# Starting the first two column pairs together, seven products each in turns, in a split-float32 kernel

## The chip, the cores and the metric

One core of a Trainium2 chip runs the kernel. The metric is the device time of one execution in microseconds; the time before is the median of three runs, 792.79 us (792.09 to 792.79). One further execution was taken with the hardware profiler.

## What is computed

The reference takes x (2048 tokens by 512), two DFT matrix pairs and three weights, and returns a mix of two branches per token:

```python
x = A_x
g = _sigmoid((x * gate_w).sum(-1, keepdims=True))
# branch a: y = Real(DFT_seq(DFT_hidden(x)))
a = einsum("bsd,ed->bse", x, dft_hid_re);  b = einsum("bsd,ed->bse", x, dft_hid_im)
y = einsum("ts,bse->bte", dft_seq_re, a) - einsum("ts,bse->bte", dft_seq_im, b)
# branch b: gate = relu(x @ W_gate), up = x @ W_up, out = (gate * up) @ W_down   (F = 1792 columns)
return g * y + (1 - g) * out
```

Everything is float32. The change lies in the first part of branch b, the products of x with `W_gate` and `W_up`.

## The kernel before

**Numbers.** TensorE multiplies values of a rounded kind (F32R). To keep float32 accuracy each operand is split into a hi part (a cast by ACT, in some places by DVE) and a lo part (operand minus hi, a subtraction on DVE), and each product is made of three matmuls, the pairs in `PARTS = ((1, 0), (0, 1), (0, 0))`: lo by hi, hi by lo, hi by hi. So every operand costs one ACT and one DVE operation before TensorE can use it.

**Blocks.** Where it can, the kernel multiplies two by two block matrices with seven products in place of eight (`LEFT`, `RIGHT`: which sums of blocks go into product m). For branch b the right side is x transposed: its blocks "11", "21", "12", "22" are (half of the 512 inputs, half of the tokens of a group q), each 128 partitions by 2 by 512. The left side is a pair of columns c of the weights (two 128-column tiles of `W_gate` and of `W_up`; seven pairs in all): four blocks, for gate and up (index i). Product 1 is block 11 by block 11, product 2 is block 12 by x's "21", products 3 to 7 need sums or differences on at least one side: 5 needs x "12" minus "11" and a weight sum, 6 adds x "22", and so on. The class `Weights` (line 403) loads and splits a pair's weights; `Block` (line 478) runs the seven products of one pair and one token group in the order 1, 5, 6, 2, 7, 3, 4, each 12 matmuls (i, inner half k, part), 84 in all. `evac` reads the banks between them: ACT copies what product 1 left into a second pair of banks, where 6 and 7 add to it, ACT keeps copies for later sums, and DVE forms h = relu(gate) times up. The eight PSUM banks are four pairs named x, m, y and t (line 342).

**The start.** The first column pair of the first token group is done in another way, by the class `Direct` (line 533): eight plain block products straight from the raw blocks, 96 matmuls, with its own copy of these weights (`wf`). It starts with 15 matmuls on a constant tile (`warm_up`, line 978) while the first loads travel. Then x's blocks come in the order "11", "21" (each in two halves, between pieces of `wf`), "12", "22", then the weights of pair 1 (`w1`, lines 985 to 1013). Meanwhile DVE and ACT split pair 1's weights and build x's sums for `Block(1, 0)`, the next in the `sequence` (line 1018). Its split weights are stored to HBM (`keep`) through POOL's queue and fetched again for the second token group at the end of branch b's first part. Then follow pairs 2 to 6 for both token groups, the spectral blocks, the two pairs left over (`tail`), the down projection (`Down`) and the sequence transform (`Sequence`, `Joint`).

**What sets the order.** Nothing is issued as it is written. Every operation is put down with a key (`op`, `pe`: `plan.now` counts matmuls), and `Plan` (lines 128 to 274) sorts the operations by key, gives DVE's and ACT's a due time from what TensorE needs, and lays them out with a small cost table (0.22667 us per matmul, 2.5 us for a landing, and so on). This fixes the order of each engine's instructions; on the chip each engine then runs its list in order and waits on semaphores. All loads go through SP's queue, at most eight at a time; stores go through POOL's. All compute instructions stand on the one source line 125, so the profile is read by tile names: `xb11h` and `xb11l` are hi and lo of x's block "11", `wf0h` the direct weights, `wa`, `wb` the split weights of products 1, 2, 4 and of 5, 6, 7, 3, `ws` and `xs` the sums, `ps` PSUM.

Of the kernel before, what the change touches and what calls it, by code (L numbers as in the profile page):

```python
# [14 lines left out]
P = 128  # L15
# [11 lines left out]
ORDER = (1, 5, 6, 2, 7, 3, 4)  # L27
BANK = {1: "x", 2: "x", 5: "m", 3: "m", 6: "y", 7: "y", 4: "t"}
# [99 lines left out]
class Plan:  # L128
# [4 lines left out]
    MATMUL, WAIT, LANDING = 0.22667, 0.035, 2.5  # L133
# [56 lines left out]
    def order(self):  # L190
# [12 lines left out]
        while any(todo.values()):  # L203
# [74 lines left out]
def kernel(ctx: ExitStack, tc, xP, xG, wf, wgu, wd, cr, ci, wri, gw, out):  # L278
# [34 lines left out]
    wb = hbm("wb", 8, P, 4, 2, P)  # L313
# [87 lines left out]
    SLOT = {1: 0, 2: 1, 4: 2, 5: 0, 6: 1, 7: 2, 3: 3}  # L401

    class Weights:
        def __init__(self, c):
            self.c = c
            self.raw = [buf(f"wr{i}", [4, 2, P]) for i in range(2)]
            self.sum = [buf(f"ws{i}", [4, 2, P]) for i in range(2)]
            self.a = [[buf(f"wa{i}{x}", [3, 2, P], F32R) for x in "hl"] for i in range(2)]
            self.b = [[buf(f"wb{i}{x}", [4, 2, P], F32R) for x in "hl"] for i in range(2)]

        def load(self, i):
            load(self.raw[i].all, wgu[self.c, i])

        def a_hi(self, i):
            E().scalar.copy(self.a[i][0].all, self.raw[i][:, :3])

        def a_lo(self, i):
            E().vector.tensor_sub(self.a[i][1].all, self.raw[i][:, :3], f32(self.a[i][0].all))

        def b_sum(self, i):  # L420
            r, o = self.raw[i], self.sum[i]
            E().vector.tensor_add(o[:, 0], r[:, 3], r[:, 2])
            E().vector.tensor_sub(o[:, 1], o[:, 0], r[:, 0])
            E().vector.tensor_sub(o[:, 2], r[:, 0], r[:, 3])
            E().vector.tensor_sub(o[:, 3], r[:, 1], o[:, 1])

        def b_hi(self, i):
            E().scalar.copy(self.b[i][0].all, self.sum[i].all)

        def b_lo(self, i):  # L430
            E().vector.tensor_sub(self.b[i][1].all, self.sum[i].all, f32(self.b[i][0].all))

        def keep(self, key):
            for n, t in enumerate(y for x in (self.a, self.b) for i in x for y in i):
                k = t.shape[0]
                op(key + 3 * n, lambda n=n, t=t, k=k: store(wb[n, :, :k], f32(t.all)))

        def fetch(self, key):
            for n, t in enumerate(y for x in (self.a, self.b) for i in x for y in i):
                k = t.shape[0]  # L440
                op(key + 6 * n, lambda n=n, t=t, k=k: load(f32(t.all), wb[n, :, :k]))

        def of(self, m, i):
            return [t[:, SLOT[m]] for t in (self.a if m in (1, 2, 4) else self.b)[i]]

    def w_prep(w, key, ahead=66):
        for i in range(2):
            op(key - ahead + 6 * i, w.load, i)
            op(key - 36 + 12 * i, w.a_hi, i)
            op(key - 30 + 12 * i, w.a_lo, i)  # L450
            op(key - 40 + 12 * i, w.b_sum, i)
            op(key - 34 + 12 * i, w.b_hi, i)
            op(key - 26 + 12 * i, w.b_lo, i)
# [24 lines left out]
    class Block:  # L478


        def __init__(self, q, w):
            self.q, self.w = q, w
# [48 lines left out]


    class Direct:
        def __init__(self):
            self.x = {b: [buf(f"xb{b}{x}", dtype=F32R) for x in "hl"] for b in ("11", "21", "12", "22")}

            self.raw = [buf(f"wf{d}", [2, 4, P]) for d in range(2)]
            self.w = [[buf(f"wf{d}{x}", [2, 4, P], F32R) for x in "hl"] for d in range(2)]
            self.g = [buf(f"dg{j}") for j in range(2)]
            self.h = [buf(f"h{d}") for d in range(2)]  # L540
            self.ps = {(f, j): Pair(2 * j + f) for f in range(2) for j in range(2)}

            for d in range(2):
                for k in range(2):
                    for n in range(3):
                        for i in range(2):
                            pe(2, self.products, [(d, i, f, 0, k, n) for f in range(2)])
                            if d == k == 1 and n == 2:
                                for f in range(2):
                                    op(plan.now, self.evac, f, i, 0)  # L550
            for d in range(2):
                for i in range(2):
                    for f in range(2):
                        pe(6, self.products, [(d, i, f, 1, k, n) for k in range(2) for n in range(3)])
                        if d == 1:
                            op(plan.now, self.evac, f, i, 1)
            h_out(0, 0, self.h, plan.now + 200)

        def products(self, all):
            for d, i, f, j, k, n in all:  # L560
                first = d == k == n == 0
                a, b = PARTS[2 - n]
                mm(self.ps[f, j][i], self.w[d][a][:, k, 2 * i + f], self.x["12"[d] + "12"[j]][b][:, k],
                   start=first, stop=d == k == 1 and n == 2)

        def w_load(self, d, k, n=slice(0, 4)):
            load(self.raw[d][:, k, n], wf[d, :, k, n])

        def w_split(self, d, k, n=slice(0, 4)):
            hi, lo = self.w[d]  # L570
            E().scalar.copy(hi[:, k, n], self.raw[d][:, k, n])
            E().vector.tensor_sub(lo[:, k, n], self.raw[d][:, k, n], f32(hi[:, k, n]))

        def x_split(self, b, k=slice(0, 2), hi=None):
            x, raw = self.x[b], piece[0, b]
# [575 lines left out]
```

## Time and profile before

| what | value |
|---|---|
| median of the runs shown | 792.79 us |
| the profiled execution's own time | 792.87 us |
| its span on the core | 790.8 us |
| granted TensorE clock over the span | 0.998 |
| matmuls in the trace | 3447 |
| HBM read, written | 123.99 MB, 60.83 MB |

The span is what the trace covers; the execution's time has about 2 us beside it. Engines are PE (TensorE), PEld (its weight loads), DVE, ACT, POOL and SP. In a timeline row stand the start, the duration, engine and line, the operation, out<-in with the shape, the count, and in brackets how long the engine was idle before it and what ended that. In a table by stage each row gives a window, then busy time and count for PE, PEld, DVE, ACT and POOL, the granted clock, the share of the DMA engines and GB/s.

### The profile page before, as it was taken

Reading aid. Unit: us, or ns where it says so; the run is one execution under the profiler, and the core shown is the slowest. Engines: PE = TensorE matmul, PEld = TensorE weight load, DVE = VectorE, ACT = ScalarE, POOL = GpSimd, SP = SyncE. Lnnn points to the kernel's source line nnn. Section 1 sums busy time; section 2 is a strip of 40 time slices with the busy share of each in tenths; the row PEclk is TensorE's granted clock in tenths of the full one; section 3 lists DMA queues with packets and bytes.
Section 4 is the critical chain, followed back from the end, with each engine's and each line's share of the span. In section 5 each row is a group of like instructions: output and inputs, shape, how many; then the busy total and the mean of one; then the engine's idle time right before and its main releaser. Section 6 shows DMA issues by size and latency. Waiting matters only on the chain.

```text
span 790.8 us, 9436 instructions
## 1 busy us (share of the span) xinstructions
PE 783.8 (99%) x3447; PEld 647.6 (82%) x3447; DVE 618.7 (78%) x680; ACT 388.6 (49%) x429; POOL 96.8 (12%) x143
## 2 busy tenths in 40 slices
PE   9999999999999999999999999999999999999997
PEld 8888888888888888888888888888788888878885
DVE  7987776767769314978765799967999999989963
ACT  5653333434245334576545474544747355574540
POOL 1102221212212111010000000200011001000200
PEclk9999999999999999999999999999999999999999
DMA  8615777575966984388588789859999889699914
GB/s 321 251 41 194 263 288 253 213 256 200 340 215 218 356 318 174 120 281 292 184 269 312 278 304 323 191 182 293 349 330 279 247 263 187 196 340 333 242 33 80
DMA packets 56750, 193.84 MB, mean 245 GB/s; under 512 B 6656, under 2 KB 6912, under 8 KB 56704
## 3 DMA queue, kind: packets, MB, share of 16 engines
q1 hardware_dynamic: 37840, 124.55, 45.4%
q0 software_dynamic: 18864, 68.69, 29.2%
q8 instruction: 27, 0.44, 0.2%
q14 instruction: 19, 0.16, 0.1%
HBM read 123.99 MB, written 60.83 MB: 234 GB/s over the span
## 4 chain that ended last, share of the span: by engine, by line
PE 94%; DVE 2%; issue 1%; ACT 1%; DMA 1%; SPq 0%; DVEq 0%
PE ps L125 94%; DMA wf<-wf 1%; ACT jch L125 1%; SPq L125 0%; DVE xs L125 0%; DVE ws L125 0%; DVE xl L125 0%; DVE h L125 0%; ACT ps L125 0%; DVE v L125 0%; DVE z L125 0%; DVE wb1l L125 0%; DVE wb0l L125 0%; ACT xh L125 0%; ACT js L125 0%
## 5 line engine op out<-in xcount | busy, mean ns | idle before, releaser
L125 PE MATMUL ps<-ch,lh 128*128 128x512 f32 x580 | 225.6, 389 | 0.0
L125 PE MATMUL ps<-cl,lh 128*128 128x512 f32 x580 | 225.6, 389 | 0.0
L125 PE MATMUL ps<-ch,ll 128*128 128x512 f32 x580 | 225.6, 389 | 0.0
L125 ACT CAST ch<-r 128x1024 fp32r<-128x1024 f32 x96 | 97.5, 1052 | 73.2 <-DVE r L125 60.2
L125 PEld LDWEIGHTS ps<-ch,ll 128*128 128x128 f32 x580 | 108.9, 188 | 22.7
L125 PEld LDWEIGHTS ps<-cl,lh 128*128 128x128 f32 x580 | 108.9, 188 | 22.7
L125 PEld LDWEIGHTS ps<-ch,lh 128*128 128x128 f32 x580 | 108.9, 188 | 22.4
L125 DVE TENSOR_TENSOR cl<-r,ch 128x1024 fp32r<-128x1024 f32 x96 | 114.5, 1220 | 1.1 <-ACT ch L125 0.6
L125 DVE TENSOR_TENSOR cl<-hr,ch 128x1024 fp32r<-128x1024 f32 (+1 forms) x56 | 59.4, 1087 | 18.7 <-ACT ch L125 17.0
L125 ACT ACTIVATE ps<-ps 128x1024 f32<-128x1024 f32 (+1 forms) x33 | 31.6, 956 | 84.2 <-PE ps L125 38.4
L125 ACT COPY s<-ps 128x1024 f32<-128x1024 f32 x42 | 42.6, 1014 | 54.0 <-PE ps L125 52.4
L125 ACT CAST ch<-hr 128x1024 fp32r<-128x1024 f32 (+1 forms) x56 | 51.7, 945 | 26.5 <-PE ps L125 21.2
L125 DVE TENSOR_TENSOR r<-r,r 128x1024 f32<-128x1024 f32 x48 | 57.1, 1218 | 0.0
L125 POOL DMA_DIRECT2D out<-z x23 | 17.1, 743 | 322.5 <-DVE z L125 322.5
L125 DVE TENSOR_TENSOR ll<-l,lh 128x1024 fp32r<-128x1024 f32 (+1 forms) x26 | 30.4, 1168 | 16.1 <-ACT lh L125 14.2
L125 DVE TENSOR_TENSOR u<-ps,s 128x1024 f32<-128x1024 f32 x26 | 31.6, 1220 | 12.1 <-PE ps L125 8.3
L125 DVE TENSOR_TENSOR jcl<-jc,jch 128x1024 fp32r<-128x1024 f32 x28 | 32.8, 1221 | 7.0 <-ACT jch L125 6.5
L125 ACT COPY ps<-ps 128x1024 f32<-128x1024 f32 x17 | 17.0, 998 | 40.3 <-PE ps L125 29.8
L125 PE MATMUL ps<-xh,wb0l 128*128 128x512 f32 x92 | 35.9, 390 | 0.2 <-ACT ps L125 0.2
L125 PE MATMUL ps<-xl,wb0h 128*128 128x512 f32 x92 | 35.8, 389 | 0.0
L125 PE MATMUL ps<-xh,wb1h 128*128 128x512 f32 x92 | 35.8, 389 | 0.0
L125 PE MATMUL ps<-xh,wb0h 128*128 128x512 f32 x92 | 35.8, 389 | 0.0
(219 smaller groups left out, 1404.0 us busy)
## 6 DMA issues: line engine op xcount, KB each, us to landing
hr<-hd SPq DMA_DIRECT2D x42, 512.0 KB, 4.5
r<-cr SPq DMA_DIRECT2D x32, 512.0 KB, 5.7
r<-ci SPq DMA_DIRECT2D x32, 512.0 KB, 6.0
hd<-hs POOLq DMA_DIRECT2D x28, 512.0 KB, 5.0
out<-z POOLq DMA_DIRECT2D x23, 512.0 KB, 6.7
td<-jt POOLq DMA_DIRECT2D x16, 512.0 KB, 4.2
ad<-a POOLq DMA_DIRECT2D x16, 512.0 KB, 5.1
l<-ad SPq DMA_DIRECT2D x16, 512.0 KB, 7.3
```

The source lines that it names most:

```text
L125: getattr(getattr(nc, self.engine), self.name)(*map(ap, self.a), **{k: ap(x) for k, x in self.k.items()})
```

## The change

- `Direct` goes, with its weights `wf`. Column pairs 0 and 1 of the first token group are both run as `Block`s with seven products, in turns: product 1 of pair 0, product 1 of pair 1, product 2 of pair 0, and so on, in the order 1, 2, 5, 6, 3, 7, 4 (`ORDER_S`). Each block has two pairs of PSUM banks; what was in x, m and t shares one pair.
- The loads come in the order that this needs: x "11" in two halves between two pieces of pair 0's block 11, pair 1's block 11, x "21" whole, both pairs' second blocks, x "12", both pairs' other two blocks, x "22".
- Products 1 and 2 of pair 0 go k by k, and hi by hi first (`one` with `first=2`, `n` in 2, 1, 0). x "21" is loaded in one piece and split in two halves (`x_half`).
- `Weights` keeps gate and up side by side: one tile for hi and one for lo of products 1 and 2, one tile `wd` for product 4, and `wb` in two halves. The sums are made product by product over 512 columns; a pair's sums are four DVE operations, not eight. Seven tiles are kept in HBM in place of eight.
- The planner's cost table multiplies a load's time by 2.3 if it is issued between 2.3 and 2.9 us. The warm-up matmuls write the two pairs of banks that product 1 is copied into.

```diff
 ORDER = (1, 5, 6, 2, 7, 3, 4)
+ORDER_S = (1, 2, 5, 6, 3, 7, 4)
 BANK = {1: "x", 2: "x", 5: "m", 3: "m", 6: "y", 7: "y", 4: "t"}
 FIRST = (1, 5)
...
-    MATMUL, WAIT, LANDING = 0.22667, 0.035, 2.5
+    MATMUL, WAIT, LANDING, COLD = 0.22667, 0.035, 2.5, 2.3
...
-                line = max(line, free[s.engine]) + s.work
+                line = max(line, free[s.engine]) + s.work * (self.COLD if 2.3 < t < 2.9 else 1)
...
-    wb = hbm("wb", 8, P, 4, 2, P)
+    wb = hbm("wb", 7, P, 2, 2, 2, P)
...
-    SLOT = {1: 0, 2: 1, 4: 2, 5: 0, 6: 1, 7: 2, 3: 3}
+    SLOT = {1: 0, 2: 1, 5: 0, 6: 1, 7: 2, 3: 3}
+            self.raw = [buf(f"wr{h}", [2, 2, 2, P]) for h in range(2)]
+            self.sum = [buf(f"ws{h}", [2, 2, 2, P]) for h in range(2)]
+            self.a = [buf(f"wa{x}", [2, 2, 2, P], F32R) for x in "hl"]
+            self.d = buf("wd", [2, 2, 2, P], F32R)
+            self.b = [[buf(f"wb{h}{x}", [2, 2, 2, P], F32R) for x in "hl"] for h in range(2)]
+        def load(self, h, n=slice(0, 2), k=slice(0, 2)):
+            load(self.raw[h][:, n, k], wgu[self.c, h, :, n, k])
+        def a_hi(self, n=slice(0, 2), k=slice(0, 2)):
+            E().scalar.copy(self.a[0][:, n, k], self.raw[0][:, n, k])
+        def a_lo(self, n=slice(0, 2), k=slice(0, 2)):
+            E().vector.tensor_sub(self.a[1][:, n, k], self.raw[0][:, n, k], f32(self.a[0][:, n, k]))
+        def d_hi(self):
+            E().scalar.copy(self.d[:, 0], self.raw[1][:, 0])
+        def d_lo(self):
+            E().vector.tensor_sub(self.d[:, 1], self.raw[1][:, 0], f32(self.d[:, 0]))
+        def b_sum(self, m):
+            (a, b), (c, d) = ([r[:, n] for n in range(2)] for r in self.raw)
+            o = [self.sum[n // 2][:, n % 2] for n in range(4)]
+            combine(o[SLOT[m]], *{5: (d, c, 1), 6: (o[0], a, -1), 7: (a, d, -1), 3: (b, o[1], -1)}[m])
+        def b_hi(self, h, n=slice(0, 2)):
+            E().scalar.copy(self.b[h][0][:, n], self.sum[h][:, n])
+        def b_lo(self, h, n=slice(0, 2)):
+            E().vector.tensor_sub(self.b[h][1][:, n], self.sum[h][:, n], f32(self.b[h][0][:, n]))
+        def all(self):
+            return *self.a, self.d, *self.b[0], *self.b[1]
+            for n, t in enumerate(self.all()):
+                op(key + 3 * n, lambda n=n, t=t: store(wb[n], f32(t.all)))
+            for n, t in enumerate(self.all()):
+                op(key + 6 * n, lambda n=n, t=t: load(f32(t.all), wb[n]))
+        def of(self, m, i, k):
+            if m == 4:
+                return [self.d[:, n, k, i] for n in range(2)]
+            n = SLOT[m]
+            return [t[:, n % 2, k, i] for t in (self.a if m < 3 else self.b[n // 2])]
...
+        for h in range(2):
+            op(key - ahead + 6 * h, w.load, h)
+            for m in ((5, 6), (7, 3))[h]:
+                op(key - 40 + 10 * h, w.b_sum, m)
+            op(key - 34 + 10 * h, w.b_hi, h)
+            op(key - 27 + 10 * h, w.b_lo, h)
+        op(key - 36, w.a_hi)
+        op(key - 30, w.a_lo)
+        op(key + 20, w.d_hi)
+        op(key + 26, w.d_lo)
...
-        def __init__(self, q, w):
-            self.q, self.w = q, w
+        def __init__(self, q, w, banks=PAIRS):
+            self.q, self.w, self.banks = q, w, banks
             self.g = {r: buf("g" + r, (N,)) for r in ("11", "21")}
             self.s = {m: buf(f"s{m}") for m in (5, 6)}
             self.u = {r: buf("u" + r) for r in ("12", "22")}
             self.h = [buf(f"h{d}") for d in range(2)]
+        def run(self):
             for m in ORDER:
                 for i in range(2):
                     pe(6, self.product, m, i)
                 self.evac(m, plan.now)
-            h_out(q, w.c, self.h, plan.now + (8 if plan.now > 270 else 100))
+            self.done(plan.now + (8 if plan.now > 270 else 100))
+        def done(self, key):
+            h_out(self.q, self.w.c, self.h, key)
         def product(self, m, i):
-            w, x, ps = self.w.of(m, i), X[self.q, m], PAIRS[BANK[m]]
-            n = 0
             for k in range(2):
-                for a, b in PARTS:
-                    mm(ps[i], w[a][:, k], x[b][:, k], start=m in FIRST and n == 0, stop=n == 5)
-                    n += 1
+                for n in range(3):
+                    self.one(m, i, k, n)
+        def one(self, m, i, k, n, first=0):
+            w, x, ps = self.w.of(m, i, k), X[self.q, m], self.banks[BANK[m]]
+            a, b = PARTS[n]
+            mm(ps[i], w[a], x[b][:, k], start=m in FIRST and k == 0 and n == first,
+               stop=m in (2, 3, 4, 7) and k == 1 and n == 2 - first)
         def evac(self, m, key):
-            x, y, p, t = (PAIRS[k] for k in "xymt")
+            x, y, p, t = (self.banks[k] for k in "xymt")
...
-    class Direct:
...
-            mm(ps8[:, 6, :N // 2], warm[:, :P], warm.all, start=n == 0, stop=n == WARM - 1)
+            half = slice(n % 2 * (N // 2), (n % 2 + 1) * (N // 2))
+            mm(ps8[:, (2, 3, 6, 7)[n // 2 % 4], half], warm[:, :P], warm.all, start=n in (0, 2, 4, 6), stop=True)
-    w1, direct = Weights(1), Direct()
+    ws = [Weights(c) for c in range(2)]
+    for m in (1, 2, 3, 5, 6, 7, 4):
+        x_raw(0, m)
+    halves, whole = [slice(0, 1), slice(1, 2)], slice(0, 2)
+
+    def x_half(m, k, hi=None):
+        h, l, raw = (t[:, k] for t in X[0, m])
+        (hi or E().scalar.copy)(h, raw)
+        E().vector.tensor_sub(l, raw, f32(h))
+
+    def w_half(w, n, k=whole):
+        w.a_hi(n, k)
+        w.a_lo(n, k)
+
+    for k in halves:
+        op(-99, x_load, 0, "11", k)
+        op(-99, ws[0].load, 0, halves[0], k)
+    op(-99, ws[1].load, 0, halves[0])
+    op(-99, x_load, 0, "21")
+    for w in ws:
+        op(-99, w.load, 0, halves[1])
+    op(-98, x_load, 0, "12")
+    for w in ws:
+        op(-98, w.load, 1)
+    op(-98, x_load, 0, "22")
+    op(-98, lambda: load(gwt[:], gw))
+    for k in halves:
+        op(-90, x_half, 1, k, plan.vector.tensor_copy)
+        op(-90, w_half, ws[0], halves[0], k)
+    op(-90, w_half, ws[1], halves[0])
+    op(-90, x_half, 2, halves[0])
+    op(-90, w_half, ws[0], halves[1])
+    op(-90, x_half, 2, halves[1])
+    op(-90, w_half, ws[1], halves[1])
+    for n, m in enumerate((5, 6, 3, 7, 4)):
+        key = 24 * n + 20
         for f, *a in ((x_sum, 0, m), (hi_of, X[0, m]), (lo_of, X[0, m])):
+            op(key, f, *a)
+        for w in ws:
+            if m == 4:
+                op(key, w.d_hi)
+                op(key, w.d_lo)
+            else:
+                h, i = divmod(SLOT[m], 2)
+                op(key, w.b_sum, m)
+                op(key, w.b_hi, h, halves[i])
+                op(key, w.b_lo, h, halves[i])
+
+    start = [Block(0, w, {k: Pair(2 * c + (k == "y")) for k in "xymt"}) for c, w in enumerate(ws)]
+    for m in ORDER_S:
+        for b in start:
+            if m in (1, 2) and b is start[0]:
+                for k in range(2):
+                    for n in (2, 1, 0):
+                        for i in range(2):
+                            pe(1, b.one, m, i, k, n, 2)
+            else:
+                for i in range(2):
+                    pe(6, b.product, m, i)
+            b.evac(m, plan.now)
+    for b in start:
+        b.done(plan.now + 100)
+    ws[1].keep(plan.now)
+    w = ws[1]
...
-    sequence = [(1, 0), (2, 0), (2, 1)]
+    sequence = [(2, 0), (2, 1)]
...
-            Block(q, w)
-            if (c, q) == (1, 0):
-                w.keep(plan.now - 40)
+            Block(q, w).run()
...
-        b = w.reshape(2, 2, P, KF // 2, 2, P).transpose(3, 2, 4, 0, 1, 5)
-        return np.stack([b[:, :, 0, 0], b[:, :, 0, 1], b[:, :, 1, 1], b[:, :, 1, 0]], axis=2)
+        return w.reshape(2, 2, P, KF // 2, 2, P).transpose(3, 0, 4, 2, 1, 5)
-    wgu = np.stack([blocks(wg), blocks(wu)], axis=1)
-
-    first = wgu[0][:, :, [[0, 3], [1, 2]]].transpose(2, 1, 4, 0, 3, 5).reshape(2, P, 2, 4, P)
+    wgu = np.stack([blocks(wg), blocks(wu)], axis=5)
+    wgu = np.stack([np.stack([wgu[:, 0, 0], wgu[:, 1, 0]], axis=2), np.stack([wgu[:, 1, 1], wgu[:, 0, 1]], axis=2)], axis=1)
-        "wf": laid(first),
```

More of the change, by code (lines that the diff above doesn't have):

```diff
@@ L277, with kernel @@
 @with_exitstack
-def kernel(ctx: ExitStack, tc, xP, xG, wf, wgu, wd, cr, ci, wri, gw, out):
+def kernel(ctx: ExitStack, tc, xP, xG, wgu, wd, cr, ci, wri, gw, out):
     nc = tc.nc
@@ L405, in __init__ @@
             self.c = c
[L406 to L428, printed above, removed]
@@ L530, in evac @@
                 rectified("21", 0, t, -1.0)
-    class Direct:
[L534 to L575, printed above, removed]
-            (hi or E().scalar.copy)(x[0][:, k], raw[:, k])
-            E().vector.tensor_sub(x[1][:, k], raw[:, k], f32(x[0][:, k]))
-        def evac(self, f, i, j):
-            g, ps = self.g[j][:, f], self.ps[f, j]
-            if i == 0:
-                E().scalar.activation(g, ps[0], AF.Relu)
-            else:
-                E().vector.tensor_mul(self.h[f][:, j], g, ps[1])
```

42 lines of the change are left out of this document (removed).

## The prediction

> **What bounds the kernel now.** I read the page first, then the chain that ended last in order of time.
>
> ```profile
> span 790.8 us, 9436 instructions
> ...
> PE 783.8 (99%) x3447; PEld 647.6 (82%) x3447; DVE 618.7 (78%) x680; ACT 388.6 (49%) x429; POOL 96.8 (12%) x143
> ```
> ```profile
> 0.74 0.39 SPq L125
> ...
> 4.50 6.52 DMA wf<-wf
> ...
> 33.10 519.88 PE ps L125 x2291
> ```
>
> The page alone says "TensorE is busy 99%". The chain says more: up to 33.10 us it runs through other work, the first loads among it (issued from 0.74 on), and after that through matmuls alone, 2291 of them in 519.88 us, so 0.2269 us each. From 33.10 on only the number of matmuls counts. Before it, what counts is when the operands of the first products are ready. The change acts on both. The table by stage says the same of the later part:
>
> ```profile
> 200.00:780.00 580.00, 579.52 (x2554) 478.68 (x2553) 462.74 (x468) 300.93 (x326) 60.63 (x82) 1.00 0.80 253
> ```
>
> TensorE is busy in 579.52 of 580.00 us, at a granted clock of 1.00. Now the landmarks of the stretch that is rewritten, from the timeline:
>
> ```profile
> 4.59 1.96 PE L125 MATMUL ps<-xb11h,wf0h 128*128 128x512 f32 x4
> ...
> 10.95 1.07 PE L125 MATMUL ps<-xb21h,wf1h 128*128 128x512 f32 x4
> ...
> 32.48 0.39 PE L125 MATMUL ps<-xh,wb1h 128*128 128x512 f32 x1
> ...
> 33.10 0.50 PE L125 MATMUL ps<-xh,wb0l 128*128 128x512 f32 x1 [0.23 <-ACT ps L125]
> ...
> 46.83 0.39 PE L125 MATMUL ps<-xb11h,wa0l 128*128 128x512 f32 x1
> ```
>
> The first real matmul starts at 4.59. The first one that reads x's second block is the 25th and starts at 10.95. Between 32.48 and 33.10 TensorE loses 0.62 - 0.23 = 0.39 us, waiting for ACT's copy of a bank; and since 33.10 + 60 x 0.2269 would be 46.71, another 0.12 just after it. At 46.83 the first matmul of column pair 2 starts: pairs 0 and 1 are through for the first half of the tokens. That is the point at which I compare, since nothing after it changes in kind.
>
> **Fewer matmuls.** Pair 0 is computed directly now:
>
> ```profile
> L125 PE MATMUL ps<-xb12h,wf0h 128*128 128x512 f32 x8 | 3.1, 389 | 0.0
> ...
> L125 PE MATMUL ps<-xb21h,wf1l 128*128 128x512 f32 x8 | 2.1, 389 | 0.0
> ```
>
> These are the first and the last of twelve such rows, x8 each: four blocks of x (xb11 to xb22) by three hi and lo parts. They make 96 matmuls. Seven products of 2 halves x 6 matmuls are 84. Twelve go: 12 x 0.2269 = 2.72 us, all on the path. Before 46.83 stand 96 + 84 = 180 real matmuls, after the change 168.
>
> **When the operands come.** The seven-product form wants other bytes earlier, so I worked out the queue. All loads go through SP's queue in the order of the code, with these sizes:
>
> ```profile
> x<-xP SPq DMA_DIRECT2D x4, 256.0 KB, 4.5
> wf<-wf SPq DMA_DIRECT2D x3, 256.0 KB, 6.1
> ...
> wf<-wf SPq DMA_DIRECT2D x2, 128.0 KB, 2.9
> ```
> ```profile
> 6.60 0.62 ACT L125 CAST wf0h<-wf 128x512 fp32r<-128x512 f32 x1 [1.71 <-DMA wf<-wf]
> ...
> 9.08 0.62 ACT L125 CAST xb21h<-x 128x512 fp32r<-128x512 f32 x1 [1.86 <-DMA x<-xP]
> ...
> 10.38 0.62 ACT L125 CAST xb21h<-x 128x512 fp32r<-128x512 f32 x1
> 11.03 0.69 DVE L125 TENSOR_TENSOR xb21l<-x,xb21h 128x512 fp32r<-128x512 f32 x1
> ...
> 12.31 1.06 ACT L125 CAST xb12h<-x 128x1024 fp32r<-128x1024 f32 x1 [0.65 <-DMA x<-xP]
> 12.31 1.22 DVE L125 TENSOR_TENSOR xs<-x,x 128x1024 f32<-128x1024 f32 x1
> ...
> 13.45 1.22 DVE L125 TENSOR_TENSOR xb12l<-x,xb12h 128x1024 fp32r<-128x1024 f32 x1
> 13.57 1.05 ACT L125 CAST xh<-xs 128x1024 fp32r<-128x1024 f32 x1 [0.20 <-DVE xs L125]
> ...
> 14.53 1.05 ACT L125 CAST xb22h<-x 128x1024 fp32r<-128x1024 f32 x1
> ```
>
> Three casts end a wait for a load, so their starts show landings: the fifth load (1024 KB in all) by 6.60, the sixth (1280 KB) by 9.08, the tenth (2560 KB) by 12.31. From the sixth to the tenth that is 1280 KB in 3.23 us, 0.65 us per 256 KB; from the fifth to the sixth 256 KB took 2.48 us, a hold-up of 1.83 us. The new queue also has 1024 KB in its first five loads (two halves of x's first block, two 128 KB and one 256 KB piece of weights). The sixth is x's second block whole, 512 KB. By equal bytes: 1536 KB at 9.08 + 0.65 = 9.7 us, the weights of the second product at 10.4 and 11.0, x's third block (2560 KB) at 12.3, the second weight halves at 13.6 and 14.9, x's fourth at 16.2. This load is the unknown of the sum. Without the hold-up it lands at 6.60 + 2 x 0.65 = 7.9; with a second one at 9.7 + 1.83 = 11.5. I take 9.7, since the nearest row has just those bytes and one fresh block of x behind five loads, and keep 7.9 and 11.5 for the range.
>
> The page "DMA: Bandwidth & Descriptors" of the Trainium skill (section "Measured (HBM→SBUF, 128 partitions, SWDGE, issued from GpSimd)" and the fit above it) gives about 2.0 us plus bytes at 436 GB/s, which is an estimate of 5.1 us for those 1024 KB issued from 0.7 on. The row says 6.60, so the measurement decides and the earlier landing stays a rival.
>
> **Costs per operation.** From the same rows: ACT 0.62 for 512 columns and 1.05 for 1024, DVE 0.69 and 1.22. Back to back they overlap: DVE 12.31 to 13.45 is 1.14 (0.08 less than its duration), ACT 13.57 to 14.53 is 0.96 (0.09 less). So the steps are DVE 0.61 and 1.14, ACT 0.53 and 0.96.
>
> **First product of both pairs.** 24 matmuls, as many as stand before 10.95 now, from the same first two loads. Pair 1's weights are in by 6.60; hi to 7.22, lo to 7.95, and its 13th matmul cannot come before 8.2. No loss.
>
> **Second product of pair 0.** It begins hi by hi. Its engine order, from the built program: ACT casts both halves of the second block, then the weights. From 9.7: 9.73, 10.26, 10.79, done at 11.41, so TensorE starts at 11.43 instead of 10.95: **0.48 us lost**. Lo follows hi after two matmuls and two more: x's is made at 10.37 to 11.06, in time, and the weights' at 11.59 to 12.28, against 11.43 + 4 x 0.2269 = 12.34.
>
> **Third product (m = 5), a DVE chain.** DVE stands without a gap from 10.37: four 0.61 steps (two lo of x, two lo of weights) to 12.81, the x difference to 13.95, two weight sums to 15.17 (plus 0.1, since the second reads the first), x's lo to 16.4, the weights' lo 0.69 to 17.1. TensorE is through with both second products at 11.43 + 24 x 0.2269 = 16.88: **0.2 us lost**. Then a weight sum, the h product, the next x sum, the weights' lo for pair 1: 0.61 + 0.61 + 1.14 + 0.69 after 17.05 = 20.1, while TensorE is ready at 17.1 + 2.72 = 19.8: **0.3 us lost**. The next on DVE (0.61, 1.14, 0.69) is done at 22.5 with TensorE there at 20.1 + 2.72 = 22.8; the fourth time the margin is 0.1 us (25.4 against 25.5); after that it grows past 2 us, as only one operand per product is left to make.
>
> **The sum.** Pair 1's third product starts at 20.1 with 168 - 60 = 108 matmuls left: 20.1 + 108 x 0.2269 = 44.6. Now it is 46.83. So **-2.2 us**: 2.72 from matmuls and 0.51 from the old wait at 33.10, less about 1.0 for the three new ones.
>
> **What costs nothing, and what covers it.** Pair 1's split weights are stored for later: the same 3.5 MB, now seven stores instead of eight, some 25 us later on POOL, so they leave the crowded start for this stretch:
>
> ```profile
> 33.00:47.00 14.00, 13.90 (x61) 11.54 (x62) 12.85 (x19) 9.29 (x12) 0.55 (x1) 1.00 0.05 19
> ```
>
> The DMA engines' share is 0.05 in the stage where the first of them now go. They stand ahead of the first h stores on POOL's queue, but those are read only by the down stage, after all other column pairs; were they late there, TensorE would show it in the 579.52 us stage, which has room in DMA (0.80). In every later pair DVE makes four sums of 512 instead of eight of 256 and ACT moves the same columns; under a TensorE without gaps this buys nothing. The warm-up's other banks keep the same 15 matmuls.
>
> The profiled execution took 792.87 us, 2.07 beside its span; less 2.2 is 790.65. The median of the runs shown is 792.79, 0.08 lower, so I forecast **790.6 us**.
>
> **Rivals.**
> 1. *The hold-up in the early loads is absent* and x's second block lands at 7.9. Then x's third block and the second weight half (12.3 and 13.6) set the third product, TensorE waits there some 0.5 us in all instead of 1.0 with the second product's, and the gain is about 2.7: 790.1. For it: the block is one 512 KB load. Against: the row at 9.08.
> 2. *A second hold-up, or a thinner DVE chain than worked out.* Weights of pair 1 are a region not read before, so 11.5 is possible: +1.8, so 792.4. Or the 15 DVE steps up to 20.1 do not overlap by 0.08: +1.2, so 791.8. Together "little gained". Against the second: the rows 12.31 and 13.45.
> 3. *Slower: x's second block lands past 11.9.* Everything from the second product on hangs on this one load through ACT and the DVE chain, one to one, so the 2.2 us are gone at 9.7 + 2.2. With two more hold-ups (13.4) it is +1.5: 794.3. TensorE then stands idle from 10.95 to 15.1, and if its pace falls back to that of the 4.59 row (four in 1.96 us, 0.49 each) for twelve matmuls, it is 12 x (0.49 - 0.23) = 3.1 more: 797.4. For it: the trace has one such hold-up in six loads, and the row at 4.59 shows the slow pace. Against: none in the loads up to 12.31, and it takes three before x lands.
>
> The 0.39 us wait at 33.10 did not slow the matmuls after it (2291 of them at 0.2269), and the waits that I forecast are as short. The page "TensorE: Matmul & The Clock Gate" of the Trainium skill ("What's actually happening") says that the array falls back to half its clock after at least one idle window of about 3.4 us. By that rule only a wait like the third rival's 4.2 us would do it; no row here shows such a wait.
>
> **How the numbers follow.** Forecast 0.55 (790.1 to 791.1, x between 9.2 and 10.2), first rival 0.16, second 0.22, third 0.07. A measurement of this kernel tells about 0.2%, 1.6 us, from no change: up to 791.2 counts as faster, up to 794.4 as the same. Forecast and first rival are faster, the second is "same", and the third I count as slower, since its price is at that bound or past it: 0.71, 0.22, 0.07. The range runs from 789.9, just under the first rival, to 792.4, the dearer end of the second.
>
> **What would show it.** Right: first matmul of column pair 2 near 44.6; the cast of x's second block at 9.7 after a wait for its load; TensorE gaps near 11, 17 and 20 us of 0.2 to 0.5 and none after; 3435 matmuls. Wrong: that cast past 10.5, DVE with gaps between 10.4 and 20 us, or TensorE waits that were not there between 45 and 550 us.

## The result, and the profile after

The changed kernel takes **790.56 us** (median of ten executions, 789.88 to 791.83), the kernel before 792.48 beside it on the same chip (792.09 to 792.91). The ratio is 0.9975 with a 95% interval of 0.9966 to 0.9985: faster by 1.9 us, or 0.25%. The forecast was 790.6.

From the page of the changed kernel, the span and part 1:

```profile
span 788.1 us, 9404 instructions
...
PE 780.7 (99%) x3435; PEld 644.7 (82%) x3435; DVE 620.4 (79%) x663; ACT 390.4 (50%) x436; POOL 96.1 (12%) x142
```

There are 3435 matmuls, twelve fewer. PE's busy time is 3.1 us shorter and the span 2.7 us. This execution, of 789.88 us, was the fastest of the ten; the median of their spans is 788.8. The time beside the span is shorter too: 1.77 us here and 1.8 in the median of the ten, where the kernel before has 2.1 in its trace and in the executions beside the experiments. So 0.3 of the 1.9 us lie outside the span, and no run shows what they are.

The chain that ended last, in order of time (start, length, engine):

```profile
2.59 4.14 DMA wr<-wgu
6.76 0.63 ACT wah L126
7.42 0.70 DVE wal L126
8.16 542.15 PE ps L126 x2387
```

Before, the last thing ahead of the long run of matmuls was ACT's bank copy at 33.10. Now it is the load of pair 1's weights, its cast and its subtraction, and from 8.16 on TensorE stands on the path with pauses too short for the chain to leave it. Those pauses are in the timeline (the bracket is the idle time before an instruction and what ended it):

```profile
7.42 0.69 DVE L126 TENSOR_TENSOR wal<-wr,wah 128x512 fp32r<-128x512 f32 x1 [0.62 <-ACT wah L126]
...
8.16 0.50 PE L126 MATMUL ps<-xh,wal 128*128 128x512 f32 x1 [0.41 <-DVE wal L126]
...
9.16 1.14 ACT L126 CAST xh<-x 128x512 fp32r<-128x512 f32 x2 [0.37 <-DMA x<-xP]
...
10.79 0.85 PE L126 MATMUL ps<-xh,wah 128*128 128x512 f32 x3
...
11.66 0.70 POOL L126 DMA_DIRECT2D wb<-wah  x1 [11.21 <-ACT wah L126]
...
16.31 0.39 PE L126 MATMUL ps<-xh,wah 128*128 128x512 f32 x1
16.66 0.47 PE L126 MATMUL ps<-xh,wb0l 128*128 128x512 f32 x1
...
19.51 0.50 PE L126 MATMUL ps<-xh,wb0l 128*128 128x512 f32 x1
19.85 0.40 PE L126 MATMUL ps<-xl,wb0h 128*128 128x512 f32 x1
...
44.16 0.39 PE L126 MATMUL ps<-xh,wal 128*128 128x512 f32 x1
```

Matmuls that follow each other without a pause start 0.23 us apart. Row by row:

- 8.16 is pair 1's first matmul, the 13th of all; it needs the weights' lo. TensorE was ready 0.57 us earlier, and 0.11 more is lost to the next matmul at 8.50.
- At 10.79 three matmuls stand in one row: the last of the first products and the first of the second product follow without a pause.
- From 16.31 to 16.66 is 0.35, so 0.12 is lost, and 0.08 more just after (the third product of pair 0). From 19.51 to 19.85 is 0.34: 0.11 lost.
- At 44.16 column pair 2 begins. Before, that was 46.83: 2.67 us sooner.

The stage that follows has no pause left, as the table by stage shows (window, length, busy time and count of PE, PEld, DVE, ACT, POOL, granted clock, DMA share, GB/s):

```profile
20.00:44.00 24.00, 24.00 (x108) 19.81 (x107) 23.84 (x31) 15.80 (x21) 3.70 (x7) 1.00 0.44 173
```

**A second trace of each kernel** says how much of 2.67 is the kernel's own. Of the kernel before:

```profile
32.32 0.39 PE L125 MATMUL ps<-xh,wb1h 128*128 128x512 f32 x1
32.55 0.39 PE L125 MATMUL ps<-xh,wb0l 128*128 128x512 f32 x1
...
46.15 0.39 PE L125 MATMUL ps<-xb11h,wa0l 128*128 128x512 f32 x1
```

Of the changed kernel:

```profile
4.71 1.22 PE L126 MATMUL ps<-xh,wah 128*128 128x512 f32 x2
...
7.39 0.63 PE L126 MATMUL ps<-xh,wah 128*128 128x512 f32 x2
...
8.98 1.00 ACT L126 COPY ps<-ps 128x1024 f32<-128x1024 f32 x1 [1.84 <-PE ps L126]
...
9.07 2.96 SPq L126 DMA_DIRECT2D x<-xP  x4
...
9.89 1.14 ACT L126 CAST xh<-x 128x512 fp32r<-128x512 f32 x2
...
17.39 0.47 PE L126 MATMUL ps<-xh,wb0l 128*128 128x512 f32 x1
...
44.87 0.39 PE L126 MATMUL ps<-xh,wal 128*128 128x512 f32 x1
```

In the second trace of the kernel before the wait at the bank copy is gone (32.32 to 32.55 is 0.23), and pair 2 begins at 46.15. In that of the changed kernel it begins at 44.87. The means are 46.49 and 44.52: 1.97 us apart. So one trace of each overstates the gain, and each kernel's start moved by 0.7 us between its two traces. From pair 2 to the end of the span it is 743.9 to 744.0 us in all four, and the two executions of a kernel differ in time as their pair 2 does (0.72 for 0.68, 0.74 for 0.71). So inside the span the difference lies ahead of pair 2, and the 0.3 us beside the span come on top: the means of the four executions are 2.26 us apart, somewhat more than the 1.92 of the medians.

### The profile page after: what moved, and what is told of

Read it like the earlier page. It is cut to its first block, busy times and chain, and to the rows that moved or that the text cites. A ratio compares the mean times of both kernels' runs of the same rounds, so it can differ in the third digit from the quotient of the medians.

```text
span 788.1 us, 9404 instructions
## 1 busy us (share of the span) xinstructions
PE 780.7 (99%) x3435; PEld 644.7 (82%) x3435; DVE 620.4 (79%) x663; ACT 390.4 (50%) x436; POOL 96.1 (12%) x142
## 4 chain that ended last, share of the span: by engine, by line
PE 97%; ACT 1%; issue 1%; DMA 1%; DVE 0%; SPq 0%; DVEq 0%
PE ps L126 97%; ACT jch L126 1%; DMA wr<-wgu 1%; SPq L126 0%; DVE v L126 0%; DVE z L126 0%; ACT js L126 0%; DVE wal L126 0%; ACT wah L126 0%; ACT ps L126 0%; DVEq L126 0%
## 5 line engine op out<-in xcount | busy, mean ns | idle before, releaser
L126 ACT COPY s<-ps 128x1024 f32<-128x1024 f32 x44 | 44.6, 1014 | 52.8 <-PE ps L126 52.8
L126 DVE TENSOR_TENSOR u<-ps,s 128x1024 f32<-128x1024 f32 x28 | 34.2, 1221 | 12.4 <-PE ps L126 6.9
L126 PE MATMUL ps<-xh,wb0l 128*128 128x512 f32 x112 | 43.8, 391 | 0.0
L126 PE MATMUL ps<-xl,wb0h 128*128 128x512 f32 x112 | 43.6, 389 | 0.0
L126 PE MATMUL ps<-xh,wb0h 128*128 128x512 f32 x112 | 43.6, 389 | 0.0
L126 PE MATMUL ps<-xh,wb1h 128*128 128x512 f32 x112 | 43.6, 389 | 0.0
L126 PE MATMUL ps<-vh,xh 128*128 128x512 f32 x112 | 43.6, 389 | 0.0
L126 PE MATMUL ps<-vh,xl 128*128 128x512 f32 x112 | 43.6, 389 | 0.0
L126 PE MATMUL ps<-xh,wb1l 128*128 128x512 f32 x112 | 43.6, 389 | 0.0
```

The costliest lines, as they stand in the source:

```text
L126: getattr(getattr(nc, self.engine), self.name)(*map(ap, self.a), **{k: ap(x) for k, x in self.k.items()})
```

## The experiments

**The theories.** A, "count and chain", is the prediction's: twelve matmuls fewer are worth 12 x 0.2269 = 2.72 us, less what TensorE waits at the second and third products, where the loads and then DVE's chain are late; what is saved ahead of that chain, it takes back. The rival B puts the gain elsewhere than in the count of matmuls. A third theory, D, came from the second trace and is told behind e6. Each ratio is to the kernel before, run on the same chip.

**e1: the twelve matmuls back.** Product 1 of pair 2's block of the first token group is made twice:

```diff
                 for i in range(2):
-                    pe(6, self.product, m, i)
+                    for _ in range(2 if m == 1 and (self.w.c, self.q) == (2, 0) else 1):
+                        pe(6, self.product, m, i)
```

> The changed kernel with the first product of column pair 2 done twice (its second pass starts the bank anew, so the output stays). It puts the twelve matmuls back where TensorE has no gap. Theory A (the gain is the twelve matmuls, 2.72 us, and the old wait at 33.10 was only traded for new ones): 2.7 us longer than the changed kernel, so level with the kernel before, ratio 1.000 to 1.001. Theory B (matmuls are cheap to hide and the gain comes from the new order at the start): under 1 us longer, so still 0.998 or faster.

Measured: 793.39 us (792.99 to 793.96), ratio 1.0013 (1.0004 to 1.0022). That is 2.83 over the changed kernel. Timeline:

```profile
45.00 0.39 PE L126 MATMUL ps<-xh,wal 128*128 128x512 f32 x1
...
253.80 1.01 ACT L126 ACTIVATE ps<-ps 128x1024 f32<-128x1024 f32 x1 [1.65 <-DVE a L126]
...
254.86 0.19 PEld L126 LDWEIGHTS ps<-vh,xl 128*128 128x128 f32 x1 [0.51 <-ACT ps L126]
```

The new order of the plan brought a wait of its own, 0.25 us and 0.11 more at 254.86, so 2.83 is the twelve matmuls and about 0.36 beside them; 2.5 is left for 2.72 expected. The traces leave out what differs ahead of pair 2 and come closer: from pair 2 to the end of the span it is 746.98 us here and 743.95 and 743.98 in the changed kernel, so 3.0, of which 2.65 are the matmuls. B falls: with the count of before, the rest of the change does not pay at all, it costs about as much as it saves or a little more.

**e2: pair 0's second product lo first.**

```diff
-            if m in (1, 2) and b is start[0]:
+            if m == 1 and b is start[0]:
```

> The changed kernel with product 2 of pair 0 in the ordinary order, lo by hi first. Theory A (a DVE chain from 9.8 us on sets the third product whatever the second does): product 2 starts about 0.7 us later, near 11.7, since it needs the weights' lo, but 0.3 of it is waits at 16.7 and 19.6 that were there anyway; column pair 2 starts 0.35 us later, the ratio rises by 0.0005. Theory B (hi by hi is what makes the start work): the whole 0.7 us and more stays.

Measured: 790.63 us, ratio 0.9976 (0.9966 to 0.9986), the changed kernel's own time. Timeline:

```profile
12.01 0.50 PE L126 MATMUL ps<-xh,wal 128*128 128x512 f32 x1 [0.83 <-DVE wal L126]
...
17.35 0.39 PE L126 MATMUL ps<-xh,wah 128*128 128x512 f32 x1
17.58 0.40 PE L126 MATMUL ps<-xh,wb0l 128*128 128x512 f32 x1
...
44.80 0.39 PE L126 MATMUL ps<-xh,wal 128*128 128x512 f32 x1
```

TensorE now waits 0.83 us for the weights' lo at 12.01, and in return no more at the third product (17.35 to 17.58 is 0.23), since it comes there later. So part of the wait is only moved, as A says. Pair 2 begins at 44.80, between the changed kernel's 44.16 and 44.87; the 0.35 us that A expects shows neither there nor in the time (counted from the cast, as in the table behind e6, it is 0.4). B, with 0.7 us and more, is not borne out.

**e4: hi first for products 1, 2 and 5 of both pairs.**

```diff
-            if m in (1, 2) and b is start[0]:
+            if m in (1, 2, 5):
```

> The changed kernel with products 1, 2 and 5 of both pairs hi by hi first. The waits of the profile at 8.16 (0.7 us, for the weights' lo of pair 1), 16.7 (0.2) and 19.6 (0.1) lose their cause. Theory A (DVE has no gap from 9.8 to 25 us, so it moves the waits on): they come back near 11 and 22 to 25 us, and column pair 2 starts within 0.2 us of 44.2. Rival (each wait is its own): all of 1.0 us is gained, pair 2 starts near 43.2, 789.6.

Measured: 789.95 us (789.70 to 790.26), ratio 0.9967 (0.9954 to 0.9979). Timeline:

```profile
9.69 1.14 ACT L126 CAST xh<-x 128x512 fp32r<-128x512 f32 x2 [0.93 <-DMA x<-xP]
...
11.40 0.73 PE L126 MATMUL ps<-xh,wah 128*128 128x512 f32 x2 [0.96 <-ACT wah L126]
...
44.54 0.39 PE L126 MATMUL ps<-xh,wal 128*128 128x512 f32 x1
```

The waits at 8.16, 16.7 and 19.6 are gone, and smaller ones stand at 22.8 (0.08) and 25.4 to 25.7 (0.20). The same trace has the latest landing of x's second block, 9.66, and 1.1 us of TensorE waiting for what is made behind it. Pair 2 begins at 44.54, between the changed kernel's two traces and far from the rival's 43.2. The median is 0.6 lower than the changed kernel's, but the intervals overlap: no gain is shown.

**e3: no turns.** Pair 0 makes all its products before pair 1 begins; the side engines' keys follow. One execution.

```diff
-    for m in ORDER_S:
-        for b in start:
+    for b in start:
+        for m in ORDER_S:
...
-        key = 24 * n + 20
+        key = 12 * n + 10
```

> The changed kernel with all seven products of pair 0 ahead of those of pair 1, the loads as they are, the sums' keys moved up so that they stand ahead of their products. Theory A (each product needs new operands, and the other pair's product covers their making): product 2 waits for x's second block from 7.4 to 10.9, product 5 for the DVE chain until 17, and products that reuse a bank wait 1 to 2 us for its reading; some 12 us longer than the changed kernel, 802. Rival (the turns matter little, the loads are in time for either): within 2 us. If waits of over 3 us let the matmuls fall to 0.43 us apart for a while, 1 to 3 us more, 803 to 805.

Measured: 806.13 us, above what was expected. Pair 2 begins at 60.14, 16 us later. The timeline and the table by stage show the waits, and what comes after them:

```profile
13.46 0.73 PE L126 MATMUL ps<-xh,wah 128*128 128x512 f32 x2 [2.65 <-ACT wah L126]
...
19.98 0.47 PE L126 MATMUL ps<-xh,wb0l 128*128 128x512 f32 x1 [1.91 <-ACT xh L126]
...
21.02 0.63 PE L126 MATMUL ps<-xl,wb0h 128*128 128x512 f32 x1
21.45 0.63 PE L126 MATMUL ps<-xh,wb0h 128*128 128x512 f32 x1
```
```profile
13.40:17.50 4.10, 4.04 (x11) 3.22 (x12) 4.03 (x7) 2.48 (x5) 1.25 (x2) 0.58 1.04 411
...
20.00:24.50 4.50, 4.50 (x13) 3.49 (x14) 4.50 (x6) 2.02 (x3) 0.00 (x0) 0.62 0.88 329
24.50:28.00 3.50, 3.50 (x17) 2.86 (x16) 3.50 (x5) 1.58 (x2) 0.00 (x0) 1.00 0.28 94
```

The turns are what gives DVE its time: without them each operand has 12 matmuls (2.7 us) to be made in, not 24, and TensorE waits. After the waits of 2.65 and 1.91 us the matmuls come 0.43 us apart (21.02 to 21.45), for about three microseconds, and the windows around them show a granted clock of 0.58 and 0.62. They were 0.43 apart from the first one up to 10.18 as well, longer than in any other trace. Some 16 matmuls went slowly after the waits, 0.20 us longer each: 3.2 us. Without them it would be 802.9, near the 802 that was expected.

**e5 and e8: x's second block in the queue.** In e5 its load moves behind both pairs' second weights; in e8 it comes in two halves, the second one there:

```diff
-    op(-99, x_load, 0, "21")
+    op(-99, x_load, 0, "21", halves[0])      # e8 only
     for w in ws:
         op(-99, w.load, 0, halves[1])
+    op(-99, x_load, 0, "21")                 # e5
+    op(-99, x_load, 0, "21", halves[1])      # e8
```

> The changed kernel with x's second block loaded behind both pairs' second weights: same bytes in all, the sixth load is 256 KB of weights now, the eighth is x. If the hold-up belongs to the sixth place in the queue (whatever it is), the weights land near 9.2 and 9.5, x near 10.5, ACT then has one cast and not three after it, product 2 starts near 11.1 and its first lo product 0.3 later; pair 2 starts within 0.2 us of the changed kernel's. If it belongs to x's block, the weights land at 7.5 to 8.2, x past 11, and pair 2 starts 0.8 us or more later.

> The changed kernel with x's second block loaded in two halves, the second behind both pairs' second weights. Product 2 can start 0.4 to 0.5 us earlier where it waits. Theory A (a DVE chain through 10 to 20 us sets the third product, and its lo of the second half now comes later): products 5 wait 1.1 us near 17 instead, and pair 2 starts 0.4 to 0.7 us later than in the changed kernel. Rival (the start of product 2 is what counts): pair 2 up to 0.5 us earlier.

Measured: e5 790.15 us, ratio 0.9970 (0.9959 to 0.9981); e8 789.88 (789.50 to 790.52), ratio 0.9966 (0.9953 to 0.9978); the changed kernel beside them on this chip 790.33 (790.00 to 790.67), 0.9973 (0.9962 to 0.9984). Timelines of e5 and of e8:

```profile
10.32 1.14 ACT L126 CAST xh<-x 128x512 fp32r<-128x512 f32 x2 [0.33 <-DMA x<-xP]
...
44.09 0.39 PE L126 MATMUL ps<-xh,wal 128*128 128x512 f32 x1
```
```profile
8.03 1.00 ACT L126 COPY ps<-ps 128x1024 f32<-128x1024 f32 x1 [0.88 <-PE ps L126]
8.94 0.62 ACT L126 CAST xh<-x 128x512 fp32r<-128x512 f32 x1
9.59 0.69 DVE L126 TENSOR_TENSOR xl<-x,xh 128x512 fp32r<-128x512 f32 x1 [1.72 <-ACT xh L126]
...
43.89 0.39 PE L126 MATMUL ps<-xh,wal 128*128 128x512 f32 x1
```

My expectation for e8 fell: it was to be later by some tenths, and pair 2 begins earlier than in any trace of the changed kernel. The sixth load, now 256 KB, had landed by 7.98, and the loads behind it came 0.65 us apart. In e5 the sixth load, 256 KB of weights, landed at 8.33. In the changed kernel the sixth is 512 KB and lands at 9.14 and 9.05, so the hold-up there goes neither with the place alone nor with x's block alone. These are single traces, though, and the same load can move by as much: the sixth of the kernel before, 256 KB, landed at 9.06 in its first trace and at 8.17 in its second. With the first half in sooner, DVE's chain starts at 9.59 in place of 9.81, the third product at 16.44 in place of 16.66. The cast could have come sooner still: its load had landed by 7.98, but it starts at 8.94, behind ACT's copy of a bank (8.03 to 9.03). On time, neither kernel can be told from the changed one: the intervals overlap.

**e6: the sums in eight pieces again.** Every `b_sum` of pairs 2 to 6 is made of two operations of 256 columns, as before the change. (The text on record speaks of pair 0's second time too; that pair's sums stayed whole.)

```diff
-            combine(o[SLOT[m]], *{5: (d, c, 1), ...}[m])
+            x, y, sign = {5: (d, c, 1), ...}[m]
+            for k in range(2) if self.c > 1 else (slice(0, 2),):
+                combine(o[SLOT[m]][:, k], x[:, k], y[:, k], sign)
```

> The changed kernel with the weight sums of pairs 2 to 6 and of pair 0's second time as eight DVE operations of 256 columns again, not four of 512; the start is as it is. Theory A (under a TensorE without gaps DVE work costs nothing): same time as the changed kernel within 0.3 us, no new wait in the trace. Rival (fewer DVE operations give part of the gain): 0.5 us or more lost.

Measured: 790.25 us, ratio 0.9970 (0.9959 to 0.9981); the changed kernel beside it 790.33. The rival's loss of 0.5 us does not show; what DVE saves there is worth nothing that can be measured.

**Theory D: the pace at the start.** Until some moment after the first matmul each one takes 0.43 us, and that moment moves: in the first trace of the changed kernel full pace came at 5.05, in the second at 7.39 (its rows at 4.71 and 7.39). With the late pace, product 1 ends late, and ACT's copy of its bank (8.98 to 9.98) stands in ACT's list ahead of the casts of x's second block. The load had landed by 9.07, but the cast starts at 9.89; in the first trace it starts at 9.16, on the landing. Everything behind follows by 0.7 us: the third product at 17.39 in place of 16.66, pair 2 at 44.87 in place of 44.16. The timeline of e6 has the same two rows, the load having landed at 8.92:

```profile
8.74 1.00 ACT L126 COPY ps<-ps 128x1024 f32<-128x1024 f32 x1 [1.70 <-PE ps L126]
9.65 1.15 ACT L126 CAST xh<-x 128x512 fp32r<-128x512 f32 x2
```

Four traces have these products alike:

| trace | full pace from | load landed | cast starts | DVE's chain starts | third product | pair 2 at |
|---|---|---|---|---|---|---|
| changed kernel, first | 5.05 | 9.14 | 9.16 | 9.81 | 16.66 | 44.16 |
| e6 | 6.40 | 8.92 | 9.65 | 10.30 | 17.15 | 44.61 |
| changed kernel, second | 7.39 | 9.05 | 9.89 | 10.55 | 17.39 | 44.87 |
| e1 | 7.26 | 9.21 | 9.99 | 10.65 | 17.50 | 45.00 |

Pair 2 follows the cast, 35.0 us behind it in every one, and not the landing: e6 has the earliest. On the way the third product starts 6.85 us after DVE's first operation (6.84 in one), so DVE's chain sets it, as A says. The cast follows the landing where full pace is early, and the copy in the three where it is late. Counted from the cast, e2 is 0.4 us behind (9.40 to 44.80) and e4 0.15 ahead (9.69 to 44.54): as far as single traces go, what A expected of them.

**e10 and e11: the copy out of the way.** In e10 DVE makes this copy for the first pair instead of ACT; e11 is e8 and e10 together.

```diff
-                op(key, lambda: e.scalar.copy(y.all, x.all))
+                op(key, lambda: (e.vector.tensor_copy if self.banks is not PAIRS and self.w.c == 0 else e.scalar.copy)(y.all, x.all))
```

> The changed kernel with the bank copy after pair 0's product 1 on DVE, which stands idle there, and not on ACT, where it sits ahead of the casts of x's second block. New theory D (two traces of the changed kernel, full pace from 5.05 and from 7.40: the second starts pair 2 0.7 us later because its late matmuls hold this copy until 9.98, and the casts, DVE's chain and product 5 follow): pair 2 starts at 44.0 to 44.2 whatever the pace at the start, so the time is 0 to 0.7 us under the changed kernel's, 0.3 in the median. Rival (the landing of x's second block decides, as I had predicted): no difference at equal landings.

> x's second block in two loads, the second behind both pairs' second weights, and the bank copy on DVE as well. Theory D: with the earlier landing (8.0 and 10.0 in the trace of the halves alone) and ACT free, no wait is left at 16 to 20 us; pair 2 starts at 43.2 where the matmuls reach full pace early and 44.2 where late, 0.7 us under the changed kernel in either: 789.6, ratio 0.9963. Rival (the waits near 17 come from DVE's own work and stay): pair 2 at 43.9 or later, no better than the halves alone.

Measured: e10 790.35 us (789.99 to 791.83), ratio 0.9969 (0.9956 to 0.9982); e11 **789.49** (789.31 to 790.23), ratio 0.9957 (0.9945 to 0.9970). Timelines of e10 and of e11:

```profile
7.41 0.62 ACT L126 CAST wah<-wr 128x512 fp32r<-128x512 f32 x1 [1.41 <-DMA wr<-wgu]
...
8.80 0.50 PE L126 MATMUL ps<-xh,wal 128*128 128x512 f32 x1 [0.79 <-DVE wal L126]
...
9.06 1.14 ACT L126 CAST xh<-x 128x512 fp32r<-128x512 f32 x2 [1.04 <-DMA x<-xP]
```
```profile
8.33 0.62 ACT L126 CAST xh<-x 128x512 fp32r<-128x512 f32 x1 [1.34 <-DMA x<-xP]
8.42 1.23 DVE L126 COPY ps<-ps 128x1024 f32<-128x1024 f32 x1 [0.70 <-PE ps L126]
...
9.56 0.68 DVE L126 TENSOR_TENSOR xl<-x,xh 128x512 fp32r<-128x512 f32 x1
...
43.88 0.39 PE L126 MATMUL ps<-xh,wal 128*128 128x512 f32 x1
```

In both, ACT's cast now starts on the landing. e10's time does not show a gain, and its trace can't say why not: in it full pace came early (5.34) and the fifth load late (7.41), so it holds another wait (8.80) and not the case that the edit is for. Its pair 2 begins at 44.30, just past the 44.0 to 44.2 that D expected. e11 does not bear D out either. Its cast comes at 8.33, 0.61 us before e8's, but DVE's own copy (8.42 to 9.65) now stands ahead of DVE's chain, which starts at 9.56 where e8's starts at 9.59. Waits of 0.10 and 0.15 us are left near 16.5 and 19.3, and pair 2 begins at 43.88, where the rival had it (43.9 or later) and where e8 has it (43.89). So the copy still holds the chain: for 1.14 us on DVE (8.42 to 9.56), where copy and cast took 1.56 on ACT (8.03 to 9.59 in e8). By these rows the two traces come out level since this one had the later pace, full from 6.17 and not 5.30, so that its copy could start only at 8.42. e11 has the lowest median here. Its interval parts from that of the kernel before; from the changed kernel's (0.9966 to 0.9985) and e8's it does not.

## Why the prediction was right, and where it was not

**The number: partly luck.** The forecast was a gain of 2.2 us, from 792.79. Measured were 1.92 us here, from 792.48, and 2.33 on the chip of e5, e6 and e8 (790.33 against 792.66). So the size is right within some tenths, but that 790.6 meets 790.56 is chance: the kernel before came out 0.3 us lower than its first three runs. Besides, 0.3 of the gain lie in the time beside the span, which the prediction carried over as the 2.07 of before and which is 1.8 now; the gain inside the span is that much smaller than the times say.

**Fewer matmuls: right.** 3435 of them, and putting twelve back cost 2.83 us, or about 2.5 (2.65 by the traces) without the wait that came with them, for 2.72 worked out.

**The old wait at 33.10: mis-sized.** It was counted as 0.51 us that goes. The second trace of the kernel before does not have it, so it is there in some executions only, and half of it would have been a fairer term.

**x's second block "by equal bytes" at 9.7: this step failed.** It landed at 9.14 and 9.05. The hold-up was taken over whole from the trace of before, where 256 KB in the sixth place took 2.48 us; the 512 KB in that place here took 2.40. The hold-up was about 1.1 in the first trace, not 1.83. It is no constant of the queue: the second trace of before has the sixth load 1.39 us behind the fifth (8.17 and 6.78), a hold-up of 0.74. In the eight traces with the new kernel's first loads x's block landed between 8.92 and 9.66 (e6 and e4), so 9.7 was just past the late end. Nor does everything hang on this load one to one, as the third rival has it: it hangs on the cast, which in the later executions the bank copy holds back.

**The second product, 0.48 lost: nothing, or 0.2** (second trace 0.09 and 0.11). This follows from the landing, and from TensorE's getting there at 11.02 and 11.52, not at 10.95.

**"First product: no loss": wrong in one trace of two.** The bound was right: the 13th matmul, pair 1's first, "cannot come before 8.2", and it came at 8.16. But I had not set it against the moment at which TensorE gets there, which hangs on the pace. With full pace from 5.05 TensorE was there 0.57 early. With full pace from 7.39 it does not wait there, and pays in slow matmuls instead.

**The third product, 0.2 and 0.3 lost: right in mechanism, the second too dear.** 0.21 and 0.11 in the first trace, 0.27 and 0.13 in the second. That DVE's chain sets them is shown by the 6.85 us between its start and the third product in four traces. After 20.6 us there are none, as said.

**The end of the stretch: 44.6, measured 44.16 and 44.87.** Misses in both directions nearly cancel here, and one term was never named. The prediction lets TensorE reach the second product at 10.95 as before, and so takes over the slow start of one trace: 24 matmuls from 4.59 to 10.95 take 0.91 us more than 24 x 0.2269. In the first trace the slow matmuls cost 0.2 and not 0.91, the second product 0.48 less and the third 0.18 less; 0.68 more went at 8.16, and some 0.2 in small gaps. In the second trace the slow matmuls cost 1.3, 0.4 more than taken over, the second product 0.28 less and the third 0.1 less, and the first matmul came 0.12 later.

**The stores: half right.** Five of the seven go from 37.72 on, as said. The first two go at 11.66 and 12.63, inside the crowded start and earlier than before, since product 2 is now made early. No wait of TensorE followed.

**The rivals.** A landing at 7.9 (first rival) comes about in e8, and its price was near: 789.88 for 790.1. The third rival's mechanism, a wait and then the slow pace, did not come in this kernel, but it is e3. There the step "by that rule only a wait like the third rival's 4.2 us would do it" failed: 1.91 us did it.

**What stays open:** what makes the hold-up of the sixth load; what the 0.3 us beside the span are; and how much of the spread of the times is theory D's. The four traces go with it, and in three of them the cast starts right behind the copy. But no run changed the pace alone, the two kernels with the copy on DVE showed no gain in time that parts from the noise, and the slowest execution of the changed kernel (791.83 us, with a span of 790.1) has no trace and lies further out than D accounts for.

## What to carry to other kernels

Where TensorE never stands still, a change is worth its matmuls, and the rest of it is worth what is left of the waits at the start: follow the chain of operands through the side engines there, since a wait saved ahead of a late chain only moves. Take a second trace of each kernel before a wait of half a microsecond is entered as a term: here the one that was to go was absent in the next execution. Moving an operation off one side engine helps less where the other engine has a chain of its own behind it (e11). And a bound on when an operand is ready is half of an answer; the other half is when the engine that needs it gets there.

## What the runs showed of the hardware

- **Waits of 2.65 and 1.91 us bring the slow pace back.** In e3, between waits, matmuls 0.43 us apart begin at 14.0 and 21.0 and end near 17.5 and 24.2. The page "TensorE: Matmul & The Clock Gate" of the Trainium skill ("What's actually happening") says that activity is judged in windows of about 3.4 us that run freely, not from the kernel's start. The four moments are 3.2 to 3.5 apart, as such windows would have it, and the granted clock of e3's trace shows the steps themselves: 0.50 from 14.10 to 17.51 and from 20.92 to 24.34, 1.00 before and between, so 3.41 us each time. In the stretches of that length that ended at 14.10 and 20.92 TensorE stood still for 2.65 and for 1.91 us. So a window does not have to be idle throughout, and a wait shorter than one is enough. Waits of about 1 us (e4, at 11.40) and of 1.25 (e3, before 31.31) did not do it.
- **The end of the slow start moves.** Full pace came between 4.87 and 7.39 us in all traces but e3's, though the warm-up is the same in all. Free-running windows would give such a spread, and the clock records fit them: in the other twelve traces the granted clock then stays at 1.00 for 781.65 us, or 778.24 in one, which are 229 and 228 times 3.413. These records begin with the first step to full, so the granted clock's column says 1.00 in the slow start too, and the pace there is read from the distance of the matmuls.
- **The first loads don't land by bytes.** The sixth landed between 7.98 and 9.66 us, by size, order and execution; the five loads after it come about 0.65 us per 256 KB apart in every trace.
